# Moving the rows of one half of the partitions in falling order, in loads and stores

## The chip, the cores and the metric

The kernel runs on one core of a Trainium2 chip. The metric is the device time of one execution in microseconds: the median of several runs.

## The reference

Inputs are `u`, `v` (8 batches, 3136 positions, 256 channels) and `z` (8, 3136, 64), all float32, and three parameters of the second unit.

```python
scores = (1.0 / S) * np.matmul(z, z.transpose(0, 2, 1))
attn = np.maximum(scores, 0.0) ** 2
x = u * np.matmul(attn, v)
proj = x @ w_proj                       # 256 -> 768
x1, x2, x3 = proj[..., :D], proj[..., D:2*D], proj[..., 2*D:]
X2 = np.fft.rfft(x2, n=S, axis=1)
H = np.fft.rfft(filter_fft, n=S, axis=0)[None]
x2_conv = np.fft.irfft(X2 * H, n=S, axis=1)
out = (x1 * x2_conv * x3) @ w_out
```

The first unit is an attention with squared ReLU, gated by `u`. The second one projects to three parts, convolves the middle part over the whole sequence by a Fourier transform, multiplies the three and projects back.

## The kernel before

**How positions lie on the partitions.** The sequence of 3136 positions is seen as 64 x 49: position = 49 n1 + n2 (`rows_n1`, L367). A tile is 128 partitions: the lower 64 hold n1 = 0 to 63 at n2 = t, the upper 64 the same n1 at n2 = 25 + t. There are 25 tiles (`NT`), the last of them with the lower half only. So for a given partition, the rows of consecutive tiles are consecutive rows of 256 channels in DRAM. `halves` (L370) gives the two halves, j = 0 (lower) and j = 1 (upper), each with its own transfer.

**The loads.** All go out from GpSimd (POOL), since they cast from float32 to bf16 on the way. `cast_u` (L381) loads one chunk of `u` (three or four tiles) in two transfers of 64 partitions. `cast_z` (L373) loads eight tiles of `z` in two. `load_rows` (L394) loads groups of four tiles of `v`, with a gap of 16 elements between groups in the destination; a call for several groups is one transfer per half, and the last tile's row is loaded into both halves apart from that (L405). In batch 0, `z` comes by SP in float32 (L433). Ahead of the main part POOL issues, in this order: v tiles 0 to 7, u of chunk 0, v tiles 8 to 24, some iotas and memsets for the tables of sines (L447 on), w_proj, u of chunk 1. POOL's transfers share eight semaphores in turn, and a transfer waits for the landing of the one eight earlier.

**The work.** The columns of the attention matrix go in seven chunks of 512, 384 or 448 positions (`CHUNKS`). For each, PE makes scores for pairs of tiles (L1299), ACT and DVE make ReLU and square (L1474, L1481, L1483), and PE weighs `v` with the result (L1329). The matrix is symmetric: part of it isn't computed again but transposed by DMA from the tiles of an earlier chunk ("mirrors", L1414, into M, M2e and M2o). `u` and `z` are turned by DMA transposes as well (L1158, L1202). At the end of a chunk DVE multiplies with `u` (L1527), then follow the projections (L847, L859, L893), the first step of the transform (L724), and for a whole batch its other steps, with spectra going through DRAM (L731, L754, L1031, L765), the inverse (L1063), the last projection (L1101) and the store (L1128), which is a transfer for each half. Stores, transposes and the spectra's transfers all stand in SP's queue.

**The order.** A planner in Python (`Plan`) runs when the kernel is built. It gives each task an engine and a place by assumed costs; then the order on every engine is fixed. On POOL, the loads of the next chunk and of the next batch's z and v come after a small copy (`await_x`, L392) that waits for DVE's product of the current chunk: 54 times in all.

Of the kernel before, what the change touches and what calls it, by code (L numbers as in the profile page):

```python
# [18 lines left out]
N1 = 64  # L19
# [27 lines left out]
def c_pe(*ns):  # L47
    return sum(n / 2400 + 0.003 for n in ns)
# [193 lines left out]
def kernel(  # L242
# [10 lines left out]
    nc = tc.nc  # L253

    B, S, D = u.shape
# [3 lines left out]
    NT = (N2 + 1) // 2  # L259
# [3 lines left out]
    VG = 4 * D + 16  # L263
# [68 lines left out]
    def bank(dtype=F32):  # L332
        if plan.bank is ps_s.slots:
            return ps_s.tile()[:, 0, :]
        for p in ps_o:
            if plan.bank is p.slots:
                return p.tile()
        return ps_m.tile([P, 512], F32) if dtype == F32 else ps_m.tile([P, 1024], BF16)
# [6 lines left out]
    def pe(kind, emit, cost, deps=(), takes=(), **kw):  # L345
        return job(kind, lambda e: emit(), {"PE": cost}, deps, takes, **kw)

    def on(engine, emit, cost, deps=(), takes=(), **kw):
        return job(None, lambda e: emit(), {engine: cost}, deps, takes, **kw)
# [17 lines left out]
    def rows_n1(x):  # L367
        return x.rearrange("(n1 n2) d -> n1 n2 d", n2=N2)

    def halves(lo, hi):  # L370
        return [(j, lo, min(hi, NT - j)) for j in range(2) if lo < NT - j]

    def cast_z(t, b, t0, t1):  # L373
        if t1 == NT:
            nc.gpsimd.dma_start(out=t[N1:P, t1 - 1 - t0, :], in_=rows_n1(z[b])[:, NT - 1, :])
        for j, lo, hi in halves(t0, t1):
            nc.gpsimd.dma_start(
                out=t[ds(j * N1, N1), lo - t0 : hi - t0, :], in_=rows_n1(z[b])[:, NT * j + lo : NT * j + hi, :]
            )

    def cast_u(b, c):  # L381
        u_nat[b, c] = t = un_p.tile()
        t0, t1 = C0[c] // P, -(-(C0[c] + CHUNKS[c]) // P)
        if t1 == NT:
            nc.gpsimd.memset(t[N1:P, t1 - 1 - t0, :], 0.0)
        for j, lo, hi in halves(t0, t1):
            nc.gpsimd.dma_start(  # L387
                out=t[ds(j * N1, N1), lo - t0 : hi - t0, :], in_=rows_n1(u[b])[:, NT * j + lo : NT * j + hi, :]
            )

    def await_x(xt):
# [2 lines left out]
    def load_rows(t, src, t0=0, t1=NT):  # L394
        r = rows_n1(src)
        g0, g1 = t0 // 4, t1 // 4
        for j in range(2):
            a = NT * j
            nc.gpsimd.dma_start(
                out=t[ds(j * N1, N1), ds(g0 * VG, (g1 - g0) * VG)].rearrange("p (g x) -> p g x", x=VG)[:, :, 0 : 4 * D],  # L400
                in_=r[:, a + 4 * g0 : a + 4 * g1, :].rearrange("p (g t) d -> p g (t d)", t=4),
            )
        if t1 == NT:
            for j in range(2):
                nc.gpsimd.dma_start(out=t[ds(j * N1, N1), ds(g1 * VG, D)], in_=r[:, NT - 1, :])  # L405
# [25 lines left out]
    for t0, t1 in zip(z_cuts, z_cuts[1:]):  # L431
        for j, lo, hi in halves(t0, t1):
            nc.sync.dma_start(  # L433
                out=zf[t0 // 16][ds(j * N1, N1), lo % 16 : lo % 16 + hi - lo, :], in_=zr[:, NT * j + lo : NT * j + hi, :]
# [60 lines left out]
    for i, (t0, t1) in enumerate(zip(z_cuts, z_cuts[1:])):  # L495
        step_ = -(-(t1 - t0) // -(-(t1 - t0) // 8))
        for g0 in range(t0, t1, step_):
            nt = min(step_, t1 - g0)
# [214 lines left out]
    def tile_rows(t0, nt):  # L713
        return P if t0 + nt - 1 < NT - 1 else N1
# [43 lines left out]
    def load_c(src, t0, nt, deps, home):  # L758
        rows = P
        box = {}  # L760

        def go():
            box["t"] = home.tile([P, 4, D], BF16)
            view = src[ds(t0 * P, (nt - 1) * P + rows), :].rearrange("(t p) d -> p t d", t=nt)
            nc.sync.dma_start(out=box["t"][:rows, 0:nt, :], in_=view)  # L765

        if home is l_p:
            return in_order(on("SP", go, 0.45, [*deps, *((d, ISSUED) for d in loads[-1:])], [l_p.slots], moves=0.4 * nt, late=LATE_C)), box
        return on("SP", go, 0.45, deps, [home.slots], moves=0.4 * nt), box
# [5 lines left out]
    for t0 in range(0, NT, 2):  # L775
        nt = min(2, NT - t0)
# [6 lines left out]
    for qq in range(NQ // 4):  # L783
# [16 lines left out]
        for i in range(4):  # L800
# [14 lines left out]
            a = pe("FB", mm, c_pe(D, D), [tb, ld], [ps_m.slots])  # L815
# [230 lines left out]
    def add_end(b, lasts, gtasks, tg, kind="FB", src=l_p, dsts=(o_p,), late=0, behind=(), then=()):  # L1046
        for t0, nt in tg:
            rows = tile_rows(t0, nt)
            dst = dsts[t0 // 4 % len(dsts)]
            ld, cb = load_c(D2[b % 2], t0, nt, lasts, src)  # L1050
            yb = {}
            ys = []
            w = (nt - 1) * P + rows
            firsts = []
            for dh in range(2):
                box = {}

                def mm(dh=dh, t0=t0, nt=nt, rows=rows, box=box, yb=yb, cb=cb):
                    box["p"] = bank()
                    if dh == 0:  # L1060
                        yb["y"] = y_p.tile()
                    for i in range(nt):
                        nc.tensor.matmul(  # L1063
                            box["p"][:, ds(i * P, rows)], cb["t"][:, i, ds(dh * P, P)], T4[:, :rows],
                            start=True, stop=True,
                        )

                def ev(dh=dh, t0=t0, w=w, box=box, yb=yb):
                    for o, n, gv in gate_views(b, dh, t0 * P, w):
                        nc.vector.tensor_tensor(yb["y"][:, dh, ds(o, n)], box["p"][:, ds(o, n)], gv, ALU.mult)  # L1070

                a = pe(
                    kind, mm, c_pe(*[rows] * nt), [ld, t4_done, *firsts, *(e for _, e in gtasks), *then],
                    [ps_m.slots] + ([y_p.slots] if dh == 0 else []),
                )
                firsts = [a]
                if dh == 0:
                    y0 = a
                else:
                    a.frees.append((ld, 0))  # L1080
                pieces = sum(1 for c in range(NC) if max(t0 * P, C0[c]) < min(t0 * P + w, C0[c] + CHUNKS[c]))
                e_ = on("DVE", ev, 0.068 * pieces + w * 0.00104, [a], prio=late)
                e_.frees.append((a, 0))
                ys.append(e_)
                for c in range(NC):
                    end = C0[c] + CHUNKS[c]
                    if t0 * P < end <= t0 * P + w:
                        e_.frees.append((gtasks[2 * c + dh][0], 1))
            ob = {}
            oe = []  # L1090
            for i0 in range(0, nt, 2):
                n = min(2, nt - i0)
                box = {}

                def mo(i0=i0, n=n, rows=rows, box=box, yb=yb, ob=ob, dst=dst):
                    box["p"] = bank()
                    if i0 == 0:
                        ob["o"] = dst.tile([P, 4, D], F32)
                    for i in range(n):
                        for k in range(2):  # L1100
                            nc.tensor.matmul(  # L1101
                                box["p"][:rows, ds(i * D, D)], yb["y"][:, k, ds((i0 + i) * P, rows)], wo16[:, k, :],
                                start=(k == 0), stop=(k == 1),
                            )

                def eo(e, i0=i0, n=n, rows=rows, box=box, ob=ob):
                    copy(
                        e, ob["o"][:rows, ds(i0, n), :].rearrange("p t d -> p (t d)"), box["p"][:rows, 0 : n * D]
                    )

                a = pe(
                    kind, mo, c_pe(*[D] * (2 * n)), [*ys, *firsts],
                    [ps_m.slots] + ([dst.slots] if i0 == 0 else []),
                )
                firsts = [a]
                if i0 == 0:
                    o0 = a
                if i0 + n == nt:
                    a.frees.append((y0, 1))
                e_ = job(None, eo, both(n * D), [a], prio=late)  # L1120
                e_.frees.append((a, 0))
                oe.append(e_)

            def store(t0=t0, nt=nt, rows=rows, ob=ob):
                r = rows_n1(out[b])
                for j in range(rows // N1):
                    a = t0 + NT * j
                    nc.sync.dma_start(out=r[:, a : a + nt, :], in_=ob["o"][ds(j * N1, N1), 0:nt, :])  # L1128

            s_ = on("SP", store, 1.3, [*oe, *behind], prio=1, moves=0.45 * nt)  # L1130
            s_.frees.append((o0, 1))

# [308 lines left out]
    for gi, g in enumerate(groups):  # L1441
        deps = []
        for un in g:
            b, c, k = un
            if b == 0:
                hi = max((plans[b, c][k][1][-1] + 1) * P, C0[c] + CHUNKS[c])
# [17 lines left out]
        for i, un in enumerate(g):  # L1464
            b, c, k = un
# [152 lines left out]
```

## Time and profile before

| | |
|---|---|
| median of 3 runs | 1051.44 us (1051.41 to 1056.19) |
| profiled execution: its span | 1056.2 us |
| mean granted TensorE clock in it | 0.990 |
| busy: PE, ACT, DVE, POOL | 1002.7, 930.4, 841.3, 175.9 us |
| packets on SP's queue (q1), share of 16 engines | 301,824; 59.8% |
| packets on POOL's queue (q0), share of 16 engines | 23,344; 20.9% |
| moved by DMA | 168.35 MB, 159 GB/s |
| u: transfers, median time from issue to landing | 112; 4.7 us |
| v: the same for tiles in groups (L399) | 86; 4.3 us |

The profile is of one execution on the chip; its span runs from the first to the last instruction and is its own time. In the lines shown below, a line of the chain is "start, duration, what", both in microseconds; a line of the timeline also has, in brackets, how long the engine had stood idle and what ended that. A digit in a strip of 40 is the busy share of one fortieth of the span, in tenths. The trace also has a record of each DMA packet: its queue, start, duration and size; the size is that of the bytes written, so a load that casts reads twice as much.

### The profile page before, as it was taken

Reading aid. Unit: us, or ns where it says so; the run is one execution under the profiler, and the core shown is the slowest. Engines: PE = TensorE matmul, PEld = TensorE weight load, DVE = VectorE, ACT = ScalarE, POOL = GpSimd, SP = SyncE. Lnnn points to the kernel's source line nnn. Section 1 sums busy time; section 2 is a strip of 40 time slices with the busy share of each in tenths; the row PEclk is TensorE's granted clock in tenths of the full one; section 3 lists DMA queues with packets and bytes.
Section 4 is the critical chain, followed back from the end, with each engine's and each line's share of the span. In section 5 each row is a group of like instructions: output and inputs, shape, how many; then the busy total and the mean of one; then the engine's idle time right before and its main releaser. Section 6 shows DMA issues by size and latency. Waiting matters only on the chain.

```text
span 1056.2 us, 18580 instructions
## 1 busy us (share of the span) xinstructions
PE 1002.7 (95%) x6335; PEld 511.0 (48%) x6335; DVE 841.3 (80%) x1449; ACT 930.4 (88%) x1326; POOL 175.9 (17%) x355
## 2 busy tenths in 40 slices
PE   5899999999999999999999999999999999999984
PEld 2443444445444544454455444545455444554573
DVE  7976678986889778997789958888788887889673
ACT  7897799997999989997999989989998899889772
POOL 3031301221022120212021310121112120001000
PEclk9999999999999999999999999999999999999997
DMA  9489836889698787898799767997789968786486
GB/s 180 74 165 162 153 76 148 151 158 178 163 162 164 136 177 168 189 154 126 169 204 180 135 139 147 181 202 130 148 163 198 179 129 158 158 187 123 115 247 202
DMA packets 325263, 168.35 MB, mean 159 GB/s; under 512 B 232766, under 2 KB 295230, under 8 KB 325168
## 3 DMA queue, kind: packets, MB, share of 16 engines
q1 hardware_dynamic: 301824, 136.19, 59.8%
q0 software_dynamic: 23344, 30.97, 20.9%
q8 instruction: 50, 0.82, 0.3%
q14 instruction: 45, 0.37, 0.1%
HBM read 90.26 MB, written 53.05 MB: 136 GB/s over the span
## 4 chain that ended last, share of the span: by engine, by line
PE 72%; DVE 9%; DMA 8%; ACT 6%; issue 3%; SPq 1%; POOL 1%; DVEq 0%; ACTq 0%; POOLq 0%
PE ps_o_t L1329 37%; PE ps_s_t L1299 11%; DMA M_t<-A_t 5%; PE ps_m_t L893 3%; PE ps_m_t L859 3%; PE ps_m_t L1101 3%; PE ps_m_t L847 3%; ACT R_t L1474 3%; PE ps_m_t L724 2%; PE ps_m_t L1001 2%; PE ps_m_t L1063 2%; DVE xT_t L1527 2%; PE ps_m_t L943 2%; DVE xh L967 1%; DMA specf<-s_t 1%
## 5 line engine op out<-in xcount | busy, mean ns | idle before, releaser
L1474 ACT ACTIVATE R_t<-ps_s_t 128x1024 f32<-128x1024 f32 (+2 forms) x552 | 488.5, 922 | 34.5 <-PE ps_s_t L1299 26.2
L1329 PE MATMUL ps_o_t<-A_t,v_t 128*128 128x512 bf16 (+2 forms) x2064 | 475.1, 355 | 1.9 <-DVE A_t L1483 1.5
L1329 PEld LDWEIGHTS <-v_t 128*128 128x128 bf16 x2688 | 253.9, 98 | 215.9 <-issue 42.2
L1483 DVE TENSOR_TENSOR A_t<-R_t 128x1024 bf16<-128x1024 f32 (+3 forms) x276 | 298.9, 1090 | 32.2 <-ACT R_t L1474 21.3
L1481 ACT ACTIVATE A_t<-R_t 128x768 bf16<-128x768 f32 (+3 forms) x276 | 257.1, 949 | 10.4 <-DMA M_t<-A_t 7.3
L1299 PE MATMUL ps_s_t<-zT_t 64*128 64x512 bf16 (+2 forms) x1088 | 155.1, 357 | 4.5 <-ACT R_t L1474 4.3
L392 POOL COPY tick<-xT_t 1x1 bf16<-1x1 bf16 x54 | 26.6, 492 | 778.7 <-DVE xT_t L1527 778.7
L1527 DVE SCALAR_TENSOR_TENSOR xT_t<-ps_o_t,uT_t 128x384 bf16<-128x384 f32 (+2 forms) x128 | 69.9, 557 | 26.2 <-PE ps_o_t L1329 16.6
L354 ACT ACTIVATE x_t<-ps_m_t 128x512 bf16<-128x512 f32 (+3 forms) x139 | 73.7, 549 | 17.0 <-PE ps_m_t L847 14.0
L1070 DVE TENSOR_TENSOR yT_t<-ps_m_t,gate_t 128x128 bf16<-128x128 f32 (+4 forms) x166 | 63.1, 425 | 27.3 <-PE ps_m_t L1063 27.1
L1299 PEld LDWEIGHTS <-zT_t 64*128 64x128 bf16 x1088 | 33.1, 94 | 103.2 <-issue 102.3
L865 DVE TENSOR_TENSOR gate_t<-ps_m_t,x_t 128x512 bf16<-128x512 f32 (+2 forms) x110 | 65.6, 618 | 20.0 <-PE ps_m_t L859 16.8
L1329 PE MATMUL ps_o_t<-M_t,v_t 128*128 128x384 bf16 (+2 forms) x336 | 77.8, 345 | 3.3 <-DMA M_t<-A_t 3.3
L358 DVE CAST x_t<-ps_m_t 128x512 bf16<-128x512 f32 (+3 forms) x90 | 54.6, 621 | 22.4 <-PE ps_m_t L893 13.4
L967 DVE TENSOR_TENSOR xh<-xh,H 98x1024 bf16<-98x1024 bf16 x112 | 72.3, 684 | 0.0
L387 POOL DMA_DIRECT2D un_t<-in_u_dram x112 | 59.7, 551 | 6.9 <-issue 4.6
L847 PE MATMUL ps_m_t<-xT_t,wp 128*128 128x512 bf16 (+2 forms) x224 | 57.5, 353 | 2.5 <-DVE xT_t L1527 1.4
L893 PE MATMUL ps_m_t<-wp,xT_t 128*128 128x256 bf16 x392 | 58.2, 273 | 1.5 <-DVE gate_t L865 1.4
L859 PE MATMUL ps_m_t<-xT_t,wp 128*128 128x512 bf16 (+2 forms) x220 | 55.5, 355 | 0.4 <-DVE gate_t L865 0.2
L354 ACT ACTIVATE xh<-ps_m_t 98x512 bf16<-98x512 f32 x86 | 50.5, 614 | 3.7 <-PE ps_m_t L943 2.5
L1329 PE MATMUL ps_o_t<-M2e_t,v_t 128*128 128x512 bf16 (+1 forms) x192 | 51.7, 370 | 1.1 <-DVE xT_t L1527 1.1
L358 DVE CAST s_t<-ps_m_t 128x512 bf16<-128x512 f32 (+2 forms) x66 | 41.4, 630 | 12.6 <-PE ps_m_t L724 10.9
(168 smaller groups left out, 1026.2 us busy)
## 6 DMA issues: line engine op xcount, KB each, us to landing
out_dram<-ost_t SPq DMA_DIRECT2D x82, 256.0 KB
spec_in_t<-spec SPq DMA_DIRECT2D x64, 196.0 KB
spec<-gs_t SPq DMA_DIRECT2D x60, 196.0 KB
spec<-s_t SPq DMA_DIRECT2D x80, 128.0 KB
v_t<-in_v_dram POOLq DMA_DIRECT2D x80, 128.0 KB, 4.1
spec_in_t<-spec SPq DMA_DIRECT2D x39, 256.0 KB
un_t<-in_u_dram POOLq DMA_DIRECT2D x56, 128.0 KB, 4.9
un_t<-in_u_dram POOLq DMA_DIRECT2D x56, 96.0 KB, 4.5
```

Source lines behind the costliest of these rows:

```text
L354: nc.scalar.activation(out_, in_, AF.Copy)
L358: nc.vector.tensor_copy(out_, in_)
L847: nc.tensor.matmul(box["p"][:, :cw], wp16[:, k, ds(nb * P, P)], xt["t"][:, k, :cw], start=(k == 0), stop=(k == 1),)
L859: nc.tensor.matmul(box["p3"][:, :cw], wp16[:, k, ds((4 + nb) * P, P)], xt["t"][:, k, :cw], start=(k == 0), stop=(k == 1),)
L893: nc.tensor.matmul(box["p"][:rows, ds(k_ * D, D)], xt["t"][:, k, ds((i + k_) * P, rows)], wp16[:, k, ds(D, D)], start=(k == 0), stop=(k == 1),
L967: nc.vector.tensor_tensor(xb["z"][:KR, i], xb["z"][:KR, i], H[:KR, qq, i], ALU.mult)
L1299: nc.tensor.matmul(ps[:m, i, :cw], zt[h, ds(t * P, m)], zt[h, ds(C0[c], cw)], start=True, stop=True)
L1329: nc.tensor.matmul(o, row(v16[b], t)[:, ds(dh * P, P)], x, start=(k == 0 and i == 0), stop=(last and i == len(pair) - 1),)
L1474: nc.scalar.activation(box["R"][:rows, 0:n, :cw], live[un][:rows, 0:n, :cw], AF.Relu)
L1481: nc.scalar.activation(a, r, AF.Square)
L1483: nc.vector.tensor_tensor(a, r, r, ALU.mult)
L1527: nc.vector.scalar_tensor_tensor(x, f, inv_s2, ut, ALU.mult, ALU.mult)
```

## The change

Loads of `u`, `v` and `z` and stores of the output name the rows of the lower half of the partitions in falling order, on both sides of the transfer. Each row still goes to the place that it had. In `load_rows`, where a falling order can't go over a gap, the transfer of the lower half is cut into one for each group of four tiles. The upper half, the first batch's `z`, the last tile's row of `v`, the filter and the weights are loaded as before.

```diff
+    def turned(x, j):
+        return x[:, ::-1] if j == 0 else x
...
@@ cast_z, cast_u (z here, u in the same way)
             nc.gpsimd.dma_start(
-                out=t[ds(j * N1, N1), lo - t0 : hi - t0, :], in_=rows_n1(z[b])[:, NT * j + lo : NT * j + hi, :]
+                out=turned(t[ds(j * N1, N1), lo - t0 : hi - t0, :], j),
+                in_=turned(rows_n1(z[b])[:, NT * j + lo : NT * j + hi, :], j),
             )
@@ load_rows
         for j in range(2):
             a = NT * j
-            nc.gpsimd.dma_start(
-                out=t[ds(j * N1, N1), ds(g0 * VG, (g1 - g0) * VG)].rearrange("p (g x) -> p g x", x=VG)[:, :, 0 : 4 * D],
-                in_=r[:, a + 4 * g0 : a + 4 * g1, :].rearrange("p (g t) d -> p g (t d)", t=4),
-            )
+            o = t[ds(j * N1, N1), ds(g0 * VG, (g1 - g0) * VG)].rearrange("p (g x) -> p g x", x=VG)[:, :, 0 : 4 * D]
+            i = r[:, a + 4 * g0 : a + 4 * g1, :]
+            if j:
+                nc.gpsimd.dma_start(out=o, in_=i.rearrange("p (g t) d -> p g (t d)", t=4))
+                continue
+            o, i = o.rearrange("p g (t d) -> p g t d", d=D), i.rearrange("p (g t) d -> p g t d", t=4)
+            for g in range(g1 - g0):
+                nc.gpsimd.dma_start(out=turned(o[:, g], 0), in_=turned(i[:, g], 0))
@@ store
-                    nc.sync.dma_start(out=r[:, a : a + nt, :], in_=ob["o"][ds(j * N1, N1), 0:nt, :])
+                    nc.sync.dma_start(out=turned(r[:, a : a + nt, :], j), in_=turned(ob["o"][ds(j * N1, N1), 0:nt, :], j))
```

More of the change, by code (lines that the diff above doesn't have):

```diff
@@ L387, in cast_u @@
             nc.gpsimd.dma_start(
-                out=t[ds(j * N1, N1), lo - t0 : hi - t0, :], in_=rows_n1(u[b])[:, NT * j + lo : NT * j + hi, :]
+                out=turned(t[ds(j * N1, N1), lo - t0 : hi - t0, :], j),
+                in_=turned(rows_n1(u[b])[:, NT * j + lo : NT * j + hi, :], j),
             )
```

## The prediction

> **What bounds the kernel now.** I read the page's engine shares first, then the chain that ended last, then the start and one load burst in the chain and the timeline, and last the trace's packet records sorted by queue and size.
>
> ```profile
> PE 1002.7 (95%) x6335; PEld 511.0 (48%) x6335; DVE 841.3 (80%) x1449; ACT 930.4 (88%) x1326; POOL 175.9 (17%) x355
> DMA  9489836889698787898799767997789968786486
> ...
> PE 72%; DVE 9%; DMA 8%; ACT 6%; issue 3%; SPq 1%; POOL 1%; DVEq 0%; ACTq 0%; POOLq 0%
> ```
>
> PE sets the end almost everywhere: 95% busy, 72% of the chain. The DMA engines run at 80 to 90% in most slices. POOL is free for 83% of the span, so time of its own costs nothing except where somebody waits for it. One such place is the start, in the chain of 0 to 30 us:
>
> ```profile
> 1.51 1.34 POOL v_t L399 x2
> 2.86 1.06 POOL un_t L387 x2
> 3.92 1.25 POOL v_t L399 x2
> 5.17 1.07 POOL v_t L405 x2
> 6.24 0.29 POOL yT_t L447
> ...
> 6.56 0.48 DVE spec_in_t L612 x2
> ...
> 8.91 0.27 PE ps_m_t L629
> ```
>
> Eight load issues stand on POOL ahead of the iota of L447. DVE waits for the iota (L612), ACT for DVE, and the transpose L629 stands in PE's queue ahead of the first scores. Whatever is added before the iota delays the whole kernel. The timeline of POOL shows how fast these loads land:
>
> ```profile
> 8.67 0.52 POOL L387 DMA_DIRECT2D un_t<-in_u_dram  x1 [0.53 <-DMA v_t<-in_v_dram]
> 9.59 0.52 POOL L387 DMA_DIRECT2D un_t<-in_u_dram  x1 [0.40 <-DMA un_t<-in_u_dram]
> ```
>
> POOL's loads share eight semaphores in turn; the ninth load waits until the first has landed, and so on. The tenth was held by the second (landed about 8.6), the eleventh by the third (9.55). The second place is the chain's DMA part: seven mirror transposes of 6 to 8 us (47.6 us in all), four of them here, from the chain in order of time:
>
> ```profile
> 250.57 7.45 DMA M_t<-A_t
> ...
> 372.46 6.04 DMA M_t<-A_t
> ...
> 495.80 6.03 DMA M_t<-A_t
> ...
> 616.59 7.07 DMA M_t<-A_t
> ```
>
> In each of the seven stretches POOL's loads are running. In the one at 616.59 the packet records show 128 packets of 2 KB and 67 of 512 B on POOL's queue between 617.25 and 620.25, and on SP's queue 34 of a transpose's 256 B packets, where 530 started in the half microsecond from 616.25 to 616.75 (at 373 to 375: 94 of 2 KB against 14).
>
> **The change, part by part.** Rows are turned on both sides of a transfer, so data and places stay the same. But a run that falls in order cannot be merged with its neighbour: a row of 4 x 256 floats that was one piece of 4 KB becomes four of 1 KB. The built program shows it (64x1024 becomes 64x4x256, 64x512 of z becomes 64x8x64) for the lower half alone, with PE, DVE, ACT and SP in the same order as before. POOL gets 284 loads for 279, because a load of v over several groups of four tiles is now one load per group: four of these five stand ahead of the iota, since 64x2x1024 becomes two and 64x4x1024 becomes four.
>
> Packet durations, medians of this trace. POOL's queue, by bytes written: 2048 B 173 ns, 1536 B 135, 1024 B 98, 512 B 60, 128 B 32. SP's queue: 4096 B 172, 1024 B 46. So a turned row costs: u or v of four tiles 4 x 60 - 173 = 67 ns; u of three 3 x 60 - 135 = 45; z 8 x 32 - 98 = 158; a store 4 x 46 - 172 = 12.
> - u: 32 loads x 64 rows x 67 + 24 x 64 x 45 = 206 us of engine time.
> - v: 48 x 64 x 67 = 206 us.
> - z (batches 1 to 7; the first comes by SP unturned): 21 x 64 x 158 = 212 us.
> - stores: 48 x 64 x 12 = 37 us.
>
> In all 661 us, over 16 engines 41 us, or 3.9% of the span on 81% that are used. Packets on POOL's queue go from 23,344 to about 51,300, on SP's from 301,824 to 311,000. Most of this lies beside PE's work.
>
> *Start.* Up to the third load, the engines had 320 rows x 173 ns / 16 = 3.5 us of POOL's packets to move. The twelfth load, the last ahead of the iota, must now wait for the fourth, the turned half of u: 3 turned loads x 256 x 60 / 16 + 128 x 173 / 16 = 4.3 us. That is 0.8 later, and some 0.2 more because all of z's packets now pass in between: it lands at 9.55 + 1.0 = 10.5. With 0.55 for the issue itself the iota starts at 11.1 instead of 6.17, 4.9 later. A wait of DVE for z (0.34 at 9.11) vanishes behind it: **+4.6 us**. Not less than 2.9: twelve issues of 0.52 to 0.73 instead of eight take 7.7 us for 4.7, waits or not. Not more than about 6.5: POOL's first packet started 1.5 us after the issue of 128 rows (1.51 to 3.0) and 1.0 after 64 (616.25 to 617.25), so 256 rows may start 1 us later, with the rest bound by packets. I take 4.6, since the wait for the fourth load is in the program. Nothing downstream gives it back: scores, v (last landing near 18, asked for at 18.8 + 4.6) and filter loads all move along.
>
> *Load bursts.* A burst holds the transposes for as long as its packets run. v and u each add 64 x 67 / 16 = 0.27 us, z 0.63. I take 0.54 (u and v) for each of the seven chain pieces, **+3.8 us**. From below, -6: SP's packets come in between smaller pieces (rival 2). From above, +12: with z in all seven 1.17 x 7 = 8.2, and some 4 for other bursts that lose their slack. By the landings, u's transposes (L1158) have a median slack of 4.9 us, but 4 of 56 have none, the waits of 7.5 us in SP's list. Other issues and POOL's dispatch (64 rows 0.52, 256 rows 0.68) hide in POOL's 83%; uncovered, 125 turned loads x 0.16 would be 20 us, which is in rival 3.
>
> The Trainium skill ("DMA: Bandwidth & Descriptors", section "Queues, rings and completion order") says that a DMA engine takes turns between queues by whole packets of several descriptors, not by single ones. By that rule a turn given to a turned load is four times as many pieces long, which speaks against this change and against rival 2; the stretch at 617 to 620 agrees, that at 15 to 18 (below) doesn't.
>
> *Stores at the end.* 12 turned ones after 1005, each 64 x 12 / 16 = 0.05 us: **+0.2**, at most 0.6. SP's issue took 0.3 to 0.6 us for 64 rows and for 256 or more alike, so it costs nothing.
>
> Sum: 4.6 + 3.8 + 0.2 = 8.6. The profiled execution (span 1056.2) would be 1064.8; it was one like the slowest of the three runs, while the median is 1051.44, so the median comes to **1060.0 us** (+0.8%). A measurement of this kernel can tell about 0.5%, 5.3 us, from no change.
>
> **The rivals.**
> 1. *The bursts are hidden.* PE idles for only 12.5 us between 200 and 1000, so the M_t pieces may be covered by other work up to their last tenths. Only the start remains, 2.9 to 4.9: 1055, same.
> 2. *Smaller pieces let the transposes through, not slower.* Between 15 and 18 us, 371 data packets on POOL's queue passed with 412 of 256 B on SP's: one for one. If turns go by single pieces, a transpose waits 60 ns for each of its own and not 173, in the half of a burst that is turned. Seven chain pieces would lose up to 1.8 us each (16 pieces per engine: 16 x 173 against 16 x 60 ns), 12.6; less the start's 4.6 that is -8: 1043. It decides from 0.7 us per piece on. Against it: a full mirror has 64 packets per engine, so it outlasts the burst anyway and pays the longer total.
> 3. *POOL's making of pieces is the bound.* First packet 1.0 us after 64 rows and 1.5 after 128 would be some 7 ns a row; 512 pieces of z and 256 each of u and v then land 2 to 5 us later in each burst. By the landings, 6 of u's 56 transposes have under 2 us of slack and 28 under 5; SP, which has the mirrors queued behind them, would wait 8 to 54 us longer in all. With half of that reaching PE and 5.5 at the start: +10 to +33, 1061 to 1084.
> 4. *The falling order is worse than piece sizes tell, or makes no pieces at all*: either the pieces merge (0) or HBM takes falling addresses badly. No row shows either.
>
> On rival 3, the Trainium skill (same page, section "Anatomy of one DMA — SWDGE (gpsimd) path") says that many descriptors can be emitted before the cost shows. That keeps its chance low; no run here shows it for 256 short pieces.
>
> **How the numbers follow.** Forecast (1057 to 1067) 0.50; rival 1 0.23; rival 2 0.11 (0.07 of it faster by over 0.5%); rival 3 0.13; rival 4 0.03 (0.01 to each side and 0.01 at no change). Faster 0.07 + 0.01 = 0.08, same 0.23 + 0.04 + 0.01 = 0.28, slower 0.50 + 0.13 + 0.01 = 0.64. The range leaves out the lower part of rival 2 and the upper third of rival 3: 1046 to 1076; the forecast's own is 1057 to 1067.
>
> **What would show it.** L447's iota (L456 now) near 11 us and PE's L629 (L638) about 4.6 later; a wait in POOL's list on v_t or un_t loads ahead of it; 51,300 packets on POOL's queue with its share near 24.8% for 20.9%; the long M_t pieces at 6.5 to 9 us. It would be wrong if the iota starts before 9.1, if mirrors land sooner during bursts, or if SP's waits for un_t grow past 20 us (rival 3).

## The result and the profile after

The changed kernel takes 1059.72 us in the median of 9 runs, the kernel before 1051.76 in the 9 beside it. The ratio of the runs is 1.0053, with a 95% interval of 1.0028 to 1.0077: 5.6 us slower, somewhere between 2.9 and 8.1. (The two medians lie 8.0 apart, but single runs of each kernel spread over 10 to 14 us, so the ratio counts.) The profiled execution has a span of 1064.8 us, for 1056.2 before.

Page of the changed kernel: engines, the DMA strip, the two main queues (packets, MB, share of 16 engines), and the chain's shares.

```profile
PE 1006.3 (95%) x6335; PEld 512.2 (48%) x6335; DVE 841.9 (79%) x1449; ACT 929.7 (87%) x1326; POOL 194.3 (18%) x360
...
DMA  9479836899799878897799877997789987785487
...
q1 hardware_dynamic: 311040, 136.19, 59.1%
q0 software_dynamic: 51264, 30.97, 23.6%
...
PE 75%; DVE 8%; DMA 7%; ACT 5%; issue 3%; SPq 1%; POOL 0%; DVEq 0%; ACTq 0%; POOLq 0%
```

POOL's queue moves the same bytes in 2.2 times as many packets, and its share grows from 20.9% to 23.6%. SP's queue has 9,216 packets more and no larger share. DMA's part of the chain didn't grow; it fell from 8% to 7%. So nothing here points to the later loads, where most of the new packets are. The chain of 0 to 30 us shows a cost at the start:

```profile
1.51 1.37 POOL v_t L411 x2
2.88 0.55 POOL v_t L407
3.43 8.51 DMA un_t<-in_u_dram
...
12.76 0.29 POOL yT_t L456
...
15.42 0.26 PE ps_m_t L638
```

Where the chain of before went through eight issues on POOL to the iota, it now goes through three and then through one transfer of 8.51 us: the lower half of `u`. The two last loads ahead of the iota waited, in the timeline of POOL (in brackets the idle time before and what ended it):

```profile
10.92 0.54 POOL L414 DMA_DIRECT2D v_t<-in_v_dram  x1 [3.20 <-DMA v_t<-in_v_dram]
12.23 0.53 POOL L414 DMA_DIRECT2D v_t<-in_v_dram  x1 [0.77 <-DMA un_t<-in_u_dram]
```

The iota starts at 12.76 us, 6.59 later than before, and PE's transpose of the first sine table at 15.42, 6.51 later. PE's first product with `v` starts at 21.48 for 14.97: again 6.51. The timeline of PE before (cut at 16 us) and after:

```profile
14.97 1.51 PE L1329 MATMUL ps_o_t<-A_t,v_t 128*128 128x512 bf16 x3
```

```profile
21.48 2.74 PE L1338 MATMUL ps_o_t<-A_t,v_t 128*128 128x512 bf16 x8
```

From there on the lag neither vanishes nor grows steadily. Half the way through the 6335 matmul records of both traces, the changed kernel is 6.6 us behind, after three quarters 8.4, after nine tenths 8.6. Up to 1000 us its granted clock was halved for 3.4 us four times, two of them in the second half of the run, and that of before once. The chain in order of time has five mirror transposes now:

```profile
258.85 6.59 DMA M_t<-A_t
...
502.61 5.84 DMA M_t<-A_t
...
623.21 5.96 DMA M_t<-A_t
...
705.68 4.95 DMA M_t<-A_t
...
824.16 8.29 DMA M_t<-A_t
```

The first three are the same transposes as the pieces of 7.45, 6.03 and 7.07 us of before, and all three are shorter. The other four of before are no longer on the chain, and the last two here weren't on it before, so these can't be compared.

### The profile page after: what moved, and what is told of

Read it like the earlier page. It is cut to its first block, busy times and chain, and to the rows that moved or that the text cites. A ratio compares the mean times of both kernels' runs of the same rounds, so it can differ in the third digit from the quotient of the medians.

```text
span 1064.8 us, 18585 instructions
## 1 busy us (share of the span) xinstructions
PE 1006.3 (95%) x6335; PEld 512.2 (48%) x6335; DVE 841.9 (79%) x1449; ACT 929.7 (87%) x1326; POOL 194.3 (18%) x360
## 3 DMA queue, kind: packets, MB, share of 16 engines
q1 hardware_dynamic: 311040, 136.19, 59.1%
q0 software_dynamic: 51264, 30.97, 23.6%
## 4 chain that ended last, share of the span: by engine, by line
PE 75%; DVE 8%; DMA 7%; ACT 5%; issue 3%; SPq 1%; POOL 0%; DVEq 0%; ACTq 0%; POOLq 0%
PE ps_o_t L1338 38%; PE ps_s_t L1308 11%; PE ps_m_t L902 4%; PE ps_m_t L868 4%; PE ps_m_t L856 3%; PE ps_m_t L1110 3%; DMA M_t<-A_t 3%; PE ps_m_t L733 2%; PE ps_m_t L1010 2%; ACT R_t L1483 2%; PE ps_m_t L952 2%; PE ps_m_t L1072 2%; DVE xT_t L1536 2%; DVE A_t L1492 1%; DVE xh L976 1%
## 5 line engine op out<-in xcount | busy, mean ns | idle before, releaser
L391 POOL DMA_DIRECT2D un_t<-in_u_dram x112 | 66.4, 614 | 5.7 <-issue 4.5
```

## The experiments

**One part of the change alone.** Two kernels split the change at the iotas. In the first, only the three calls ahead of them are turned; in the second, everything but these.

```diff
 def turned(x, j):
-    return x[:, ::-1] if j == 0 else x
+    return x[:, ::-1] if j == 0 and turn_now[0] else x
+turn_now = [True]                 # second kernel: False
...
 load_rows(v16[0], v[0], 8, NT)
+turn_now[0] = False               # second kernel: True
```

> Turned (and v split by groups) only in the three calls ahead of the iotas: v tiles 0 to 7, u of chunk 0, v tiles 8 to 24 of batch 0; every later load and every store as before. Theory A (the whole cost is the start): the iota of the sine tables starts near 12.8 us and PE's first transpose of a sine table near 15.4, as in the changed kernel, and the time is 6 to 7 us over before (ratio 1.006). Theory B (the prediction's sum, bursts cost 3.8): the same start, but less than the changed kernel by about 4 us.

> The complement: the three calls ahead of the iotas as before, every later load of u, v and z and every store turned. Theory A: the iota at 6.2 us, ratio 1.000, within 1.5 us of before. Theory B: 3.8 us over before (1.0036). Rival 2 (smaller pieces let the mirror transposes through): 2 us or more under before (0.998 or less).

Measured: the start alone 1062.28 us, ratio 1.0071 (1.0048 to 1.0095); all but the start 1054.87, ratio 1.0006 (0.9983 to 1.0030), both against 1054.64 of before on that chip. In the first, PE's table transpose starts at 15.12; in the second at 8.89, as before. The timeline of PE in each:

```profile
15.12 0.27 PE L641 MATMUL ps_m_t<-ident,T 128*128 128x128 bf16 x1 [10.06 <-DVE T L633]
```

```profile
8.89 0.27 PE L641 MATMUL ps_m_t<-ident,T 128*128 128x128 bf16 x1 [3.71 <-DVE T L633]
```

So the start carries the whole loss, within the intervals. The 3.8 us that the prediction gave to the bursts (1.0036) lie outside the second kernel's interval.

**The suspected cost of the bursts doubled.** The start as before, but all later transfers turned in both halves (`if j == 0 and` taken out of the condition, and `load_rows` cut by groups in both).

> The start as before (three calls ahead of the iotas unturned), but all later loads of u, v and z and all stores turned in both halves, so that what the bursts cost is doubled. Theory A: within 2 us of before (0.998 to 1.002). Theory B (3.8 us for one half): 7.6 us over before (1.007). Rival 2 (pieces let the mirror transposes through): 2 to 5 us under before (0.995 to 0.998).

Measured: 0.9998 (0.9983 to 1.0013). POOL's queue now has three times the packets of before, and the time doesn't move:

```profile
q0 software_dynamic: 75856, 30.97, 26.8%
```

This also shuts out the second rival at the sizes given.

**The wait taken away.** The iotas and memsets for the tables go ahead of all loads, in the changed kernel and in the one before:

```diff
 nc.gpsimd.iota(pi_i[:], pattern=[[0, 1]], base=0, channel_multiplier=1)
+nc.gpsimd.iota(kcol[:, 4 * N2 : 4 * N2 + P], ...)
+...                               # all iotas and memsets of kcol, 1.1 us
...
 load_rows(v16[0], v[0], 8, NT)
-nc.gpsimd.iota(kcol[:, 4 * N2 : 4 * N2 + P], ...)
-...
```

> The changed kernel with the iotas and memsets of the sine tables moved ahead of POOL's loads, so that no load stands before them; all turning kept. Theory A: the start's cost is the iotas' place behind the twelfth load, so it goes: PE's first scores by 9.5 us, and the time within 1.5 us of before (5 to 6 under the changed kernel). Theory B: 3.8 us over before. A third theory (the loads themselves come too late for PE): the first products with v still start near 21 us.

> The kernel before with the iotas and memsets moved ahead of POOL's loads, nothing turned. If the iotas' place is what sets the start: the first scores at about 6 us instead of 9.1, up to 3 us under before (0.997); if z's landing near 9.1 us sets it as well: the second batch of transposes still near 10 us and within 0.5 us of before. Which of the two is open; I take a gain of 0.5 us.

Measured: the changed kernel with its iotas first 1052.23 us, ratio 0.9970 (0.9954 to 0.9986); the kernel before with iotas first 0.9997 (0.9975 to 1.0018). The loads are as late as in the changed kernel (the last big piece of `v` lands at 17.95 us for 17.83) and still the loss is gone, so they weren't too late for PE: the iota's place was all. PE in the turned kernel with iotas first, and the transfer that its chain goes through instead:

```profile
6.36 0.27 PE L638 MATMUL ps_m_t<-ident,T 128*128 128x128 bf16 x1 [1.25 <-DVE T L630]
...
12.29 1.20 PE L535 MATMUL ps_m_t<-ident,xT_t 128*128 128x128 bf16 x9 [3.24 <-ACT xT_t L354]
```

```profile
3.94 7.33 DMA ost_t<-in_z_dram
```

The first scores come 2.6 us sooner than before, but then PE waits 3.24 us for `z`, and most of the gain is given back: the first product with `v` starts at 14.28 instead of 14.97.

**What makes the wait.** Two kernels with one run each (1063.11 and 1059.77 us; their times are not compared, only their starts). The first cuts the two loads of `v` ahead of the iota by groups and turns nothing anywhere; the second turns only the first two calls and leaves `v` tiles 8 to 24 whole (nine loads ahead of the iota).

```diff
 # first kernel
 def turned(x, j):
-    return x[:, ::-1] if j == 0 else x
+    return x
...
 load_rows(v16[0], v[0], 8, NT)
+split_now[0] = False              # later loads of v whole again
```

```diff
 # second kernel, with turn_now as above
 cast_u(0, 0)
+turn_now[0] = False
 load_rows(v16[0], v[0], 8, NT)
```

> Nothing turned anywhere; only the two loads of v ahead of the iotas are cut by groups, as in the changed kernel, so that twelve loads of 4 KB rows stand there and the twelfth waits for the fourth. Theory A1 (the wait for the fourth load's landing, and pieces make that landing late): the packets up to the fourth load are those up to the third of before, which landed at 9.3, so the iota starts near 10.1 (before 6.17, changed kernel 12.76). Theory A2 (only the number of loads counts, not the size of their pieces): the iota near 12.7. Theory A3 (POOL's own time for issues alone): near 8.5.

> Turned in the first two calls alone (v tiles 0 to 7, u of chunk 0); v tiles 8 to 24, all later loads and the stores as before. Nine loads ahead of the iotas, the ninth waits for the first, which landed at 4.8 in the changed kernel. Theory A1: no wait is left, the iota starts near 7.0 (POOL's own time for one load more and longer issues), the start costs 0.8 us. If small pieces by themselves delay the start (by taking v's or z's place in the engines): PE's first scores still 2 us or more later than before.

POOL in the first and in the second:

```profile
10.85 0.52 POOL L416 DMA_DIRECT2D v_t<-in_v_dram  x1 [0.44 <-DMA un_t<-in_u_dram]
11.37 0.28 POOL L459 IOTA yT_t<- 128x128 int32 x1
```

```profile
6.85 0.37 POOL L459 IOTA yT_t<- 128x128 int32 x1
```

With nothing turned, twelve loads put the iota at 11.37 us: 5.20 of the 6.59 come from cutting two loads into six, because the twelfth then waits for the fourth. Turning adds the last 1.39; these are single profiles, and the same start stood at 12.46 instead of 12.76 in the kernel with the start alone turned. Whether the 1.39 comes from the smaller pieces or from the falling order isn't separated. With small pieces but nine loads the iota is at 6.85, only 0.68 later than before, and PE's table transpose at 9.61, 0.70 later. So the number of loads ahead of the iota decides more than their pieces. The measured 11.37 lies halfway between theory A1 (10.1) and theory A2 (12.7): the wait for the fourth load is there, but 1.3 us longer than A1's arithmetic.

**Why the fourth load lands so late.** The changed kernel, with batch 0's `z` loaded by POOL behind the iotas, so that SP's queue is out of the way of the first loads (one run, 1069.77 us; only the start is read).

```diff
-            nc.sync.dma_start(            # z of batch 0, ahead of POOL's loads
...
 nc.gpsimd.memset(k00[:, N2 : N2 + 1], S // 2)
+            nc.gpsimd.dma_start(          # the same six transfers
```

> The changed kernel with batch 0's z loaded by POOL behind the iotas, not by SP beside the first loads, so that the loads ahead of the iotas have the DMA engines to themselves (PE of course starts later). It asks why the fourth load landed at 11.95 and not at the 10.5 of the prediction. If z's packets on SP's queue, taken in turn with the small pieces, hold it: packets alone need 4.3 us from 3.0, landing by 8.5, and the iota near 9.1. If POOL makes the pieces too slowly, or the engines are uneven by themselves: landing at 11 or later and the iota at 11.5 or later.

```profile
9.00 1.20 POOL L414 DMA_DIRECT2D v_t<-in_v_dram  x2 [1.28 <-DMA v_t<-in_v_dram]
10.21 0.28 POOL L451 IOTA yT_t<- 128x128 int32 x1
```

By the semaphore's record the fourth load lands at 9.40 instead of 11.95, and the iota starts at 10.21. So `z` beside the loads costs 2.55 us of the 12.76, in one profile each. It isn't all: packets alone were to take until 8.5. The third load, 128 rows with 1.4 us of packets over 16 engines, lands 3.1 us after the second even so (8.72 after 5.58). Of the 36 packets of 2 KB that started between 5.0 and 6.0 us, 16 took over 250 ns, up to 1432, where the median over a whole run is 173. Why is not settled.

**A faster version?** Three kernels more with the iotas first: the whole change once more, the lower half turned in all later transfers only, and both halves turned in all later transfers only.

> The kernel of e3 once more: the whole change, with the iotas ahead of POOL's loads. If 0.997 stands, it is a version faster than before by about 3 us; if scatter, 0.998 to 1.000.

> The iotas ahead of POOL's loads, the first three calls unturned, the lower half turned in all later loads and in the stores. With e11 on the same chip it asks whether the 0.3% under before of the turned kernel with iotas first came from the start (turned and split first loads) or from the later loads. If from later loads: 0.997 here as well. If it was scatter: both between 0.998 and 1.000.

> The iotas ahead of POOL's loads, the three first calls unturned, all later loads and stores turned in both halves: the two edits together that cost nothing or gained so far. If turned rows in the bursts help (the turned kernel with iotas first was 0.3% under before, the unturned one level): 0.994 to 0.997. If that gain came from the start or from scatter: 0.998 to 1.000, as with the iotas moved alone.

Measured: 0.9981 (0.9955 to 1.0007), 0.9991 (0.9967 to 1.0016) and 0.9988 (0.9974 to 1.0001). All lie a little under before, none clear of it. The whole change with iotas first is the lowest in both of its measurements, 0.9970 and 0.9981; by the quotient of the ratios it is 0.7 to 0.8% under the changed kernel, and it is at least level with the kernel before, but a gain of 2 to 3 us over the latter is shown by one interval and not by the other. If turned pieces help by a few tenths of a percent, these runs don't tell it from scatter.

## Why the prediction's time was right and two of its terms were wrong

The forecast was 1060.0 us, slower by 0.8%, with 1046 to 1076 as its range; measured were 1059.72, and by the ratio 0.53%. Of the forecast's +8.6 us the start was to give 4.6 and gave 6.5, and the bursts were to give 3.8 and gave nothing that the runs show: two errors that went opposite ways. That the time came within 0.3 us is luck besides, since 8.6 lies above the interval of 2.9 to 8.1.

- *The pieces.* POOL's packets were to be about 51,300 and SP's 311,000: they are 51,264 and 311,040. The share of POOL's queue grew by 2.7 points, not 3.9. The 3.9 counted the stores' 0.2, which are on SP's queue. The remaining 2 KB packets took less time in the mean (204 ns for 222, 0.5 points), and the rows of `z` that went had taken 135 ns in the mean, not their median of 98 (0.3 points).
- *The start, mechanism right and term mis-sized.* The twelfth load waits for the turned half of `u`, and the whole kernel moves by about what PE's table transpose moves. The term was 4.6 us and measured 6.51. 1.45 of the difference is the fourth load's landing, 10.5 against 11.95: I had carried the pace of the first three landings of before over to it and gave 0.2 us for `z`. The experiment with `z` behind puts 2.55 us on `z`, of which some part was in that pace already. Another 0.5 lies behind the landing: the iota starts 0.81 us after it, not 0.55, and 0.08 of the move vanishes on the way to PE, not 0.34. That 6.51 falls on the bound of "about 6.5" is chance, because the bound's reason, small pieces that start later, didn't occur: POOL's first packet started at 3.02 us, for 3.05 before. The prediction also spread the cause over pieces and waits; the split alone makes 5.2 of 6.6.
- *The bursts, wrong.* The step "a burst holds the transposes for as long as its packets run", with 0.54 us on each of seven chain pieces, gave +3.8. Measured is nothing: 1.0006 for one half, 0.9998 for both. The added packet time is there, but it is passed on only in part, and not to PE. Summed over the 53 to 55 bursts behind 36 us, POOL's packets take 203 to 206 us over 16 engines in the five traces with these loads unturned, 230 to 233 in the six with one half turned, and 267 and 268 in the two with both. The bursts, from first issue to last landing, take 377 to 391, 390 to 404, and 403 and 407. And the mirror transposes don't get longer: the one near 250 us, 7.45 to 7.94 in the five unturned traces, has 6.53 to 7.42 in the six turned ones whose chain it is on. The forecast pieces of 6.5 to 9 us were 6.59, 5.84 and 5.96 where they can be compared. Which part of the longer bursts PE had slack for, and which the transposes made up, stays open.
- *The stores.* From the start of the last spectrum's load to the end of the span it is 23.1 us (23.3 before): the 0.2 can't be seen.
- *Rival 1*, only the start remains, was the right picture of the time, with the start's term too small: it gave 2.9 to 4.9.
- *Rival 2* needs 0.7 us off each chain piece and a total under before. The piece near 250 us is shorter by about that (the two near 500 and 620 us are as short with the start alone turned, 5.79 and 5.90), but neither half nor both halves turned is faster beyond the interval. Within one burst the packets show both pictures: in the one at 623 of the changed kernel, 91 packets of 512 B on POOL's queue started between 624 and 625 us beside none of a transpose, and 165 beside 339 in the microsecond after.
- *Rival 3* (POOL makes the pieces too slowly) fell. In the burst at 622.86, the first packet of a turned load of 256 pieces started 1.33 us after the issue; in that at 616.25 before, with 64 rows, it was 1.23 (the prediction had read 1.0). The Trainium skill's statement in "DMA: Bandwidth & Descriptors", section "Anatomy of one DMA — SWDGE (gpsimd) path", that many descriptors can be emitted before it shows, agrees with that. SP's waits for `u` grew from 7.5 to 9.0 us in all, far from the rival's 8 to 54 more. The Trainium skill's rule on turns by whole packets is neither shown nor refuted here; the prediction's step from it, that a turn of a turned load is then four times as many pieces long, was an assumption of mine that no run tests.
- *Rival 4.* The pieces didn't merge (51,264 packets), and falling addresses cost nothing that shows in the later loads (0.9998 with both halves). At the start they may have a part in the 1.39 us that turning adds.

## What to carry to other kernels

Where an engine's queue holds short work behind transfers that take their semaphores in turn, count the transfers ahead of it: the one that goes round to a semaphore still in flight costs a landing, not an issue. Cutting two loads into six put 5.2 us on the critical start, while three times as many packets on POOL's queue later on cost nothing that the runs can tell (0.9998): the bursts grew by a third of the added packet time, and what was left didn't reach the end. So price added packets by a run in which they are doubled, not by their sum alone. Put the short work that others wait for ahead of the transfers, then look at what is next: here it was `z`, and the gain shrank from 2.6 us to 0.7.

## What the runs showed of the hardware that I had not expected

Cutting a load's rows of 4 KB into 1 KB pieces left its median time from issue to landing unchanged under load: 4.3 us for the 84 later loads of `v` in groups when both halves are turned, and 4.3 for the 86 of before. A transfer of 1.4 us of packets took 3.1 to 4.8 us to land after its forerunner in five kernels with turned or cut loads at the start, and 2.1 and 2.9 in the two runs of the kernel with the iotas ahead of the loads. And a store's 1 KB packets had a median of 69 ns in the changed kernel, where one half of the rows comes in such pieces, but 48 with both halves turned and twice as many, and 46 for the few single-row ones before; SP's queue had a share of 59.1% for 59.8 before.
